# Four small reorderings in a fused attention and two-layer kernel: weight conversion at a step's end, softmax masks ahead of the divisions, some softmax copies on ScalarE

## The chip, the cores and the metric

The kernel runs on one core of a Trainium2 chip. The metric is device time in microseconds (us); lower is better. Times are given as the median of several executions, and one further execution was recorded by the hardware profiler. Engines are named as in the profile: PE is TensorE (matmuls), PEld its weight loads, DVE is VectorE, ACT is ScalarE, POOL is GpSimd, SP the engine that issues most DMAs.

## The reference

Causal attention with a running-sum bias, then two feed-forward layers. Shapes: 4 batches, 8 heads, 576 positions, 64 per head; 2304 tokens, model width 512, hidden width 2048.

```python
scores = scale * q @ k^T                       # per batch and head
bias = -(cum[:, :, :, None] - cum[:, :, None, :])   # cum: running sum of max(s, 0)
scores = where(causal, -1e9, scores + minimum(bias, 0))
attn = exp(scores - max); attn /= sum(attn) + 1e-9
x = attn @ v                                   # to 2304 x 512
h = maximum(x @ moe_w_in, 0);  x = h * h @ moe_w_out
h = x @ moe2_w_in;  out = (h * cos(h)) @ moe2_w_out
```

## The kernel before, in words

Tokens are cut into 9 blocks of 256. Attention of block k+1 runs beside the first feed-forward layer of block k. The layer of one block is 16 chunks; for each chunk `g1` multiplies the block by a slice of `w_in` (into the PSUM tile hps), `gact` makes relu and square on ACT, `grest` on DVE makes the low half gl, and `g2` multiplies by a slice of `w_out`. A call of `g1` or of `g2` is a slot, and slots alternate: g1 of chunk n, g2 of chunk n-2, g1 of chunk n+1. After the ninth block the second layer runs alone; the change does not touch it.

The order on every engine is the order in which `step` writes instructions down, and each engine works through its own in that order. One step handles one attention job i (one head, up to 128 query rows) at several stages of its life, and one to three slots. In order: ACT `x_high`; the first slot; ACT `prep_high` (the head two further on, raw to hi); DVE `evacuate` (three small operations a pair of heads: add, reciprocal, and the product that empties the PSUM tile pvs into xp); `softmax_tail`, which is `emit_mask(i - 1)` on DVE, then `emit_split(i - 2)` (a high copy p = sb * PSC, L650 on ACT or L652 on DVE, and a low part L656 on DVE); `x_low`, `grest`; `gact` of the first slot; `c_step`; DVE `prep_low`; PE `emit_qk(i)`; the further slots; ACT `emit_exp(i - 1)`; `turn` (PE transposes xp into the PSUM tile xps, and for a block's first pair DVE reduces a scale in `x_scale`, L769, that ACT's `x_high` of the next step reads); PE `emit_pv(i - 5)`; `c_total`; DMA transposes of p; loads.

`emit_qk` writes one of three PSUM buffers, and a job of 576 keys takes two, so that its second part needs the first mask of the job before it. The last block's attention (unit 8) is 16 such jobs, each a head of its own, in the steps that run beside the layer of blocks 6 and 7.

The layer's first three blocks use `w_in` as two fp32r halves; from the fourth (k = KC) on, as two fp16 halves. `c_step` converts it, chunk by chunk, during blocks 2 and 3: `c_add` (DVE, L872), then `c_high` (ACT, L878) at least two chunks of time later, then `c_low` (DVE, L883) in the next step. The times are chunk numbers t = `slots[0][1]`, the number of the next slot's chunk; `c_add(c)` is due at 33 + int(c * CONV_PACE). Before that, in blocks 1 and 2, `c_square` (ACT, L862) takes the power of each slice; after 12 and after 16 of them `c_total` has PE sum them over rows (L836, into a few columns of xps), and `c_scales` (DVE, L849 and three more) makes scales of the sum. The transposes, the value sums (`v_sum`, L453) and these sums all write the one tile xps, one PSUM bank.

`g1` of block 3 calls `c_step` itself where a slice is not converted yet.

Of the kernel before, what the change touches and what calls it, by code (L numbers as in the profile page):

```python
# [23 lines left out]
NF = DFF // 128  # L24
# [13 lines left out]
G2LAG = 2  # L38
PASSES = ((0, 0), (0, 1), (1, 0))
KC = 3  # L40
CONV_PACE = 1.7
SQ_A = 12


def _weave(*chains):

    chains = [iter(c) for c in chains if c is not None]
    while chains:
        for c in list(chains):
            if next(c, c) is c:  # L50
                chains.remove(c)
# [49 lines left out]
def _paired(head):  # L101

    return head[4] == [64]
# [29 lines left out]
def attention_moe_moe_kernel(  # L133
# [360 lines left out]
    def v_early():  # L494
        for f, g in vq[0] if vq else ():
            if f is v_scale:
                yield from f(g)
# [99 lines left out]
    def emit_exp(i):  # L597
        n, ti, q, r = jobs[i]
        h = heads[n][2]
        j = jd[i]  # L600
        x = h % 2
        if _paired(heads[n]):
            if x == 0:
                return
            r, x = 128, 0
        w, sb = j["w"], j["sb"]
        z = pd[n - h % 2]["z"]
        nc.scalar.activation(  # L608
            out=sb[0:r, 0:w], in_=sb[0:r, 0:w], func=ACTF.Exp, scale=-1.0, bias=j["nb"],
            accum_out=z[0:r, ti, x:x + 1],  # L610
        )
        if _paired(heads[n]):
            nc.scalar.copy(z[0:64, 0, 1:2], z[64:128, 0, 0:1])
# [16 lines left out]
    def emit_split(i):  # L630
        n, ti, q, r = jobs[i]
        j = jd[i]
        if _paired(heads[n]):
            if heads[n][2] % 2 == 0:
                return
            r = 128
        w, sb = j["w"], j["sb"]
        cw = 128 * ((w + 127) // 128)
        if n < EARLY:
            pp = j["ps"][0][0][:, BT:BT + cw]  # L640
            pt = at.tile([128, 640], F32, tag="pt", bufs=3, name="pt1")
            (nc.scalar.copy if ti else nc.vector.tensor_copy)(pt[:, 0:w], pp)
            j["pt"] = pt
            yield
            return
        p = p_tile(i)
        if cw > w:
            nc.gpsimd.memset(p[0:r, 0:2 * cw].rearrange("p (a c) -> p a c", a=2)[:, :, w:cw], 0.0)
        if 0 < cdone[1] and NF - 1 not in w16 and i % 2:
            nc.scalar.activation(out=p[0:r, 0:w], in_=sb[0:r, 0:w], func=ACTF.Copy, scale=PSC)  # L650
        else:
            nc.vector.tensor_scalar(  # L652
                out=p[0:r, 0:w], in0=sb[0:r, 0:w], scalar1=PSC, scalar2=None, op0=ALU.mult
            )
        yield
        nc.vector.scalar_tensor_tensor(  # L656
            out=p[0:r, cw:cw + w], in0=sb[0:r, 0:w], scalar=PSC, in1=p[0:r, 0:w],
            op0=ALU.mult, op1=ALU.subtract,
        )
        pt = at.tile([128, 1280], F16, tag="pt", bufs=3, name="pt")  # L660
        pt = pt[:, 0:2 * cw // 128 * r].rearrange("p (a r) -> p a r", r=r)
        turned.append((pt, p[0:r, 0:2 * cw]))
        if not last_block(i):
            p_turn()
        j["pt"] = pt
        if _paired(heads[n]):
            jd[i - 1]["pt"], j["pt"] = pt[:, :, 0:64], pt[:, :, 64:128]
        yield
# [221 lines left out]
    def c_step(t, last=None):  # L890


        for c in clow:
            c_low(c)
        clow.clear()
        while chigh and (chigh[0][1] + 2 <= t or last is not None and chigh[0][0] <= last):
            c, _ = chigh.pop(0)
            while clow:
                c_low(clow.pop(0))
            c_high(c)  # L900
            clow.append(c)
        if last is not None and last in clow:
            for c in clow:
                c_low(c)
            clow.clear()
        c_scales()
        n = 0
        while cdone[0] < NF and n < 1 and t >= (
            NF + 2 + cdone[0] if cdone[0] < SQ_A else 2 * NF + 2 + 2 * (cdone[0] - SQ_A)
        ):  # L910
            c_square(cdone[0])
            cdone[0] += 1
            n += 1
        while cdone[1] < cdone[2] and t >= (KC - 1) * NF + 1 + int(cdone[1] * CONV_PACE) and (
            cdone[1] not in (1, 2) or cdone[1] - 1 in w16 and cdone[1] - 1 not in w32
        ):
            c_add(cdone[1])
            chigh.append((cdone[1], t))
            cdone[1] += 1

    def c_total():
        if cdone[0] == SQ_A and SQ_A not in csent:
            csent.append(SQ_A)
            c_sums(0, SQ_A)
        elif cdone[0] == NF and NF not in csent:
            csent.append(NF)
            c_sums(SQ_A, NF)
# [12 lines left out]
    def job(i):  # L940
        return jobs[i] if 0 <= i < NJ else None
# [7 lines left out]
    def heads_ahead(i, *fs):  # L949
        if job(i) and jobs[i][1] == 0:  # L950
            for cnt, f, d in fs:
                upto(cnt, jobs[i][0] + d, f)
# [359 lines left out]
            stages[s] += 1  # L1312
            yield stages[s] - 1

    def softmax_tail(i):
        if job(i - 1):
            yield from emit_mask(i - 1)
        for j in stage(2, i - 2):
            yield from emit_split(j)
# [6 lines left out]
    def step(moe=0, bits=0, attn=True):  # L1326

        i = prog[0]
        held = len(xtq)
        prog[0] += attn  # L1330
        if attn:
            for j in stage(1, i - 2):
                emit_exp(j)
        x_high()
        if attn and job(i - 2):
            emit_turn(i - 2)
        if attn:
            heads_ahead(i, (next_, load_ext, 2))
        w_age()
        w_scales()  # L1340
        n = moe_slot() if moe else None
        slow = bool(vq) and any(f is v_wait for f, g in vq[0])
        if slow:
            v_sums()
        if attn:
            heads_ahead(i, (nhigh, prep_high, 2))
        _weave(evacuate())
        y_evict()
        if not attn or g2done[0] < 2:
            rests()  # L1350
        if xcq and xcq[-1][-1] and xcq[-1][0] == 1:
            x_low()
        _weave(softmax_tail(i) if attn else None, w_step(bits), None if slow else v_early())
        x_low()
        rests()
        w_lows()
        if attn and job(i - 1) and jobs[i - 1][0] < EARLY:
            for j in stage(1, i - 1):
                emit_exp(j)
        act(n)  # L1360
        if moe and slots and NF < slots[0][1] < (KC + 2) * NF:
            c_step(slots[0][1])
        if attn:
            heads_ahead(i, (nlow, prep_low, 2))
        if slow:
            _weave(v_early())
        if not (attn and last_block(i)):
            y_store()
        if attn and job(i):
            emit_qk(i)  # L1370
        if attn and last_block(i):
            heads_ahead(i, (nraw, load_raw, 4))
        for _ in range(moe - 1):
            act(moe_slot())
            y_evict()
        w_sums()
        if attn:
            for j in stage(1, i - 1):
                emit_exp(j)
        behind = any(job(j) and _paired(heads[jobs[j][0]]) for j in (i - 6, i - 5))  # L1380
        if attn and not behind:
            values(i)
        turn(held if moe and i > last_job[0] + TURN_FROM else len(xtq))
        if not slow:
            v_sums()
        if attn:
            for j in stage(3, i - LAG[0]):
                if j > i - lag(j):
                    stages[3] -= 1
                    break  # L1390
                emit_pv(j)
        if attn and behind:
            values(i)
        if moe:
            c_total()
        p_turn()
        w_ahead()
        if attn:
            heads_ahead(i, (nraw, load_raw, 4))
        v_late()  # L1400
        y_store()
        if later and prog[0] >= later[0][0]:
            later.pop(0)[1]()
# [45 lines left out]
    def w_step(n):  # L1449

        js = list(range(nw[2], min(nw[2] + n, wlim[0])))
        while wlow:
            w_lo(wlow.pop(0))
            yield
        w_squares()
        while wrest and not split(wrest[0]):
            w_rest(wrest.pop(0))
        if js:
            w_clip_to(js[-1])
            for _ in zip(*[w_bits(j) for j in js]):  # L1460
                yield
            for j in js:
                if wq[j][0] == 0:
                    wrest.append(j)
                else:
                    wbit.append(j)
            nw[2] += len(js)
# [495 lines left out]
```

## Time and profile before

| | us |
|---|---|
| median of 3 executions | 970.33 |
| lowest, highest | 970.06, 972.43 |
| the profiled execution | 972.91 |
| its span, first to last instruction | 970.8 |

The granted TensorE clock was 0.998 of full speed over the span. PE is busy for 97% of it. A busy matmul includes the time in which it flows through the array, so a PE that is always busy can still be late: matmuls are better read by the distance of their starts. Attention and the first layer take the span up to about 595 us, the second layer the rest. In the profile, waits and chains name the instruction that ended a wait.

### The profile page before, as it was taken

The page shows a single profiled execution, that of the slowest core. Times are in us where ns is not written, and L with a number is a line of the kernel's source. Part 1 is how long each engine was busy: PE and PEld are TensorE (multiplying, and loading weights), DVE is VectorE, ACT ScalarE, POOL GpSimd, SP SyncE. Part 2 cuts the span into 40 slices and gives each one's busy share as a digit, 9 for nine tenths or more (in the row PEclk, how much of TensorE's full clock was granted, in tenths as well). Part 3 has the DMA queues.
Part 4 walks back from the last instruction along what each step waited for, and adds up shares of the span by engine and source line. Part 5 has one row for each costly group of instructions (what it writes and reads, how often), then busy time and mean ns, then how long its engine had stood idle before and what let it go on. Part 6 is the DMA issues. An engine that isn't in the chain of part 4 may idle for free.

```text
span 970.8 us, 21039 instructions
## 1 busy us (share of the span) xinstructions
PE 937.3 (97%) x7474; PEld 726.9 (75%) x7474; DVE 769.7 (79%) x1944; ACT 709.7 (73%) x1625; POOL 159.9 (16%) x298
## 2 busy tenths in 40 slices
PE   6999999989999999999999999999999999999997
PEld 5899998988989988999989986445544456666664
DVE  6899986789798866787997375888788788798774
ACT  6799887878898767676776686677777666565553
POOL 2001123222211222222330022430000000001101
PEclk9999999999999999999999999999999999999999
DMA  8984799657998987589999679210000000112001
GB/s 246 312 271 149 168 213 227 168 145 151 200 183 191 204 195 170 134 177 174 211 215 158 217 267 362 66 44 23 1 1 1 22 1 22 49 60 67 23 22 66
DMA packets 158074, 135.38 MB, mean 139 GB/s; under 512 B 109272, under 2 KB 132128, under 8 KB 157968
## 3 DMA queue, kind: packets, MB, share of 16 engines
q1 hardware_dynamic: 147664, 123.78, 50.8%
q0 software_dynamic: 10304, 10.24, 5.2%
q8 instruction: 59, 0.97, 0.4%
q14 instruction: 47, 0.39, 0.1%
HBM read 93.91 MB, written 15.83 MB: 113 GB/s over the span
## 4 chain that ended last, share of the span: by engine, by line
PE 59%; DVE 6%; ACT 3%; issue 2%; DMA 2%; SPq 0%; DVEq 0%; ACTq 0%
PE o L1671 18%; PE hp L1610 12%; PE y L1197 11%; PE hps L1165 9%; PE bank L1762 5%; PE qkp L567 2%; PE pvs L697 2%; DVE k L415 1%; DVE sb L585 1%; DMA raw<-in_qk_dram 1%; DMA rw<-in_w_dram 1%; DMA vb<-v_d 1%; DVE wt L1678 1%; PE xps L752 0%; ACT sb L608 0%
## 5 line engine op out<-in xcount | busy, mean ns | idle before, releaser
L1197 PE MATMUL y<-gh,wt 128*128 128x256 f32 x1152 | 237.7, 289 | 0.0
L1197 PEld LDWEIGHTS y<-gh,wt 128*128 128x128 f32 x1152 | 188.6, 190 | 1.2
L1671 PE MATMUL o<-wt,gh 128*128 128x512 f16 x576 | 171.3, 379 | 1.5 <-ACT gh L1649 1.3
L1197 PE MATMUL y<-gl,wt 128*128 128x256 f32 x576 | 162.9, 283 | 0.5 <-DVE gl L1187 0.5
L1165 PE MATMUL hps<-xh,w 128*128 128x256 f16 x1152 | 142.0, 273 | 2.6 <-ACT g L1177 2.4
L1610 PE MATMUL hp<-yh,wt 128*128 128x512 f16 (+1 forms) x448 | 124.9, 348 | 0.0
L1165 PEld LDWEIGHTS <-w 128*128 128x128 f16 x1152 | 106.1, 98 | 17.8 <-issue 4.2
L1197 PEld LDWEIGHTS y<-gl,wt 128*128 128x128 f32 x576 | 109.9, 191 | 1.4 <-DVE gl L1187 0.9
L1671 PE MATMUL o<-wt,gl 128*128 128x512 f16 x288 | 109.2, 379 | 0.0
L1610 PEld LDWEIGHTS <-wt 128*128 128x128 f16 x672 | 63.9, 98 | 59.1
L1671 PEld LDWEIGHTS <-gh 128*128 128x128 f16 x576 | 56.3, 98 | 56.3 <-ACT gh L1649 1.6
L608 ACT ACTIVATE sb<-sb 128x128 f32<-128x128 f32 (+7 forms) x152 | 87.4, 575 | 4.9 <-DVE sb L585 4.3
L1177 ACT ACTIVATE g<-hps,sc 128x256 f32<-128x256 f32 x96 | 45.1, 470 | 61.3 <-PE hps L1165 59.8
L397 POOL DMA_DIRECT2D k<-ext_d x80 | 41.1, 514 | 260.2 <-PE qkp L567 159.3
L1165 PE MATMUL hps<-xh,wt 128*128 128x256 f32 x384 | 81.4, 294 | 0.3 <-ACT g L1179 0.2
L1187 DVE TENSOR_TENSOR gl<-g,gh 128x256 fp32r<-128x256 f32 x144 | 61.3, 426 | 22.8 <-ACT gh L1181 14.7
L1610 PE MATMUL hp<-yl,wt 128*128 128x512 f16 (+1 forms) x224 | 78.0, 348 | 0.0
L585 DVE CUSTOM_DVE_ANT_0 sb<-qkp,mask 128x128 f32<-128x128 f32 (+7 forms) x152 | 69.3, 456 | 5.3 <-PE qkp L552 4.3
L656 DVE SCALAR_TENSOR_TENSOR p<-sb,p 128x384 f16<-128x384 f32 (+3 forms) x120 | 66.3, 553 | 8.8 <-ACT p L650 5.6
L1635 ACT ACTIVATE a<-kf 128x512 f32<-128x512 f32 (+1 forms) x80 | 46.5, 583 | 31.4 <-DVE kf L1630 30.4
L405 ACT CAST hi<-raw 128x704 fp32r<-128x704 f32 (+2 forms) x80 | 58.8, 735 | 13.6 <-DMA raw<-in_qk_dram 7.2
L1165 PEld LDWEIGHTS hps<-xh,wt 128*128 128x128 f32 x384 | 64.5, 195 | 2.8 <-issue 1.2
(172 smaller groups left out, 2006.8 us busy)
## 6 DMA issues: line engine op xcount, KB each, us to landing
rw<-in_w_dram SPq DMA_DIRECT2D x64, 512.0 KB
raw<-in_qk_dram SPq DMA_DIRECT2D x48, 352.0 KB
yr<-y_d SPq DMA_DIRECT2D x17, 512.0 KB
raw<-in_qk_dram SPq DMA_DIRECT2D x16, 384.0 KB
v_d<-vt SPq DMA_DIRECT2D x16, 320.0 KB
vb<-v_d SPq DMA_DIRECT2D x32, 160.0 KB
vr<-in_v_dram POOLq DMA_DIRECT2D x15, 320.0 KB, 5.4
y_d<-yst SPq DMA_DIRECT2D x18, 256.0 KB
```

The source lines that it names most:

```text
L405: nc.scalar.copy(hi[:, BT - nq:BT + nk], raw[:, BT - nq:BT + nk])
L585: nc.vector.tensor_tensor_reduce(out=sb[0:r, c0:c0 + cn], in0=p[0:r, 0:cn], in1=mask[0:r, mo:mo + cn], scale=-0.125, scalar=(3.0e38 if k = ...
L608: nc.scalar.activation(out=sb[0:r, 0:w], in_=sb[0:r, 0:w], func=ACTF.Exp, scale=-1.0, bias=j["nb"], accum_out=z[0:r, ti, x:x + 1],)
L656: nc.vector.scalar_tensor_tensor(out=p[0:r, cw:cw + w], in0=sb[0:r, 0:w], scalar=PSC, in1=p[0:r, 0:w], op0=ALU.mult, op1=ALU.subtract,)
L1165: nc.tensor.matmul(hp, w[:, a, c * 128:(c + 1) * 128], (xh, xl)[e][:, c, :], start=(n == 0), stop=(n == 3 * KD - 1),)
L1177: nc.scalar.activation(out=g, in_=hp, func=ACTF.Relu, scale=hs1[:, f // 2:f // 2 + 1])
L1187: nc.vector.tensor_tensor(out=gl, in0=g, in1=gh, op=ALU.subtract)
L1197: nc.tensor.matmul(yps[k][d // 2][:, d % 2, :], w[:, a, d * 128:(d + 1) * 128], (gh, gl)[e], start=(f == 0 and n == 0 and d % 2 == 0), sto ...
L1610: nc.tensor.matmul(hp, chunk_of(w, a, c), (yh, yl)[e][:, c, :], start=(m == 0), stop=(m == 3 * KD - 1),)
L1635: nc.scalar.activation(out=a, in_=kf, func=ACTF.Sin, scale=-6.2831850)
L1671: nc.tensor.matmul(ops[j][a], (gh, gl)[e][:, a * 128:(a + 1) * 128], w[:, x, :], start=(first and m == 0), stop=(last and m == 2),)
L1762: nc.tensor.matmul(bank[b][:, 0:HB], w[:, a, wx, c * 128:(c + 1) * 128], y_side(j, yx, e, c), start=(start and n == 0), stop=(n == 5), ski ...
```

## The change

- `c_step` moves from behind the first slot's `gact` to behind the last slot and `emit_exp`, still ahead of `values`, `turn` and `emit_pv`; `c_total` moves from the end of a step to directly ahead of `c_step`, so the sum of the squares that a step's `c_step` completes is made one step later.
- `c_step` makes at most one `c_high` and one `c_add` a call (the wait of two chunks between them stays). `CONV_PACE` is 1.6 in place of 1.7. Since t is now read behind the last slot, the chunk numbers at which an operation falls due come one step earlier or later than before.
- In steps whose first slot is a g1 of block 1 or later, `emit_mask(i - 1)` stands ahead of `evacuate`.
- In the last block, the high copy of every odd job goes to ACT.

```diff
-CONV_PACE = 1.7
+CONV_PACE = 1.6
...
-        if 0 < cdone[1] and NF - 1 not in w16 and i % 2:
+        if i % 2 and (0 < cdone[1] and NF - 1 not in w16 or last_block(i)):
             nc.scalar.activation(out=p[0:r, 0:w], in_=sb[0:r, 0:w], func=ACTF.Copy, scale=PSC)
...
-        while chigh and (chigh[0][1] + 2 <= t or last is not None and chigh[0][0] <= last):
+        while chigh and (not clow and chigh[0][1] + 2 <= t or last is not None and chigh[0][0] <= last):
...
-        while cdone[1] < cdone[2] and t >= (KC - 1) * NF + 1 + int(cdone[1] * CONV_PACE) and (
+        if cdone[1] < cdone[2] and t >= (KC - 1) * NF + 1 + int(cdone[1] * CONV_PACE) and (
...
-    def softmax_tail(i):
-        if job(i - 1):
+    def softmax_tail(i, first):
+        if job(i - 1) and not first:
             yield from emit_mask(i - 1)
...
+        first = attn and job(i - 1) and n is not None and n >= NF
+        if first:
+            _weave(emit_mask(i - 1))
         _weave(evacuate())
...
-        _weave(softmax_tail(i) if attn else None, w_step(bits), None if slow else v_early())
+        _weave(softmax_tail(i, first) if attn else None, w_step(bits), None if slow else v_early())
...
         act(n)
-        if moe and slots and NF < slots[0][1] < (KC + 2) * NF:
-            c_step(slots[0][1])
...
         if attn:
             for j in stage(1, i - 1):
                 emit_exp(j)
+        if moe and slots and NF < slots[0][1] < (KC + 2) * NF:
+            c_total()
+            c_step(slots[0][1])
...
-        if moe:
-            c_total()
```

## Rows read from the trace of the kernel before

**Rows 1.** The page, busy time: share of the span, instructions.
```profile
PE 937.3 (97%) x7474; PEld 726.9 (75%) x7474; DVE 769.7 (79%) x1944; ACT 709.7 (73%) x1625; POOL 159.9 (16%) x298
```
**Rows 2.** Waits of PE, whole span: who released it, us, times, longest.
```profile
PE qkp L567 <- DVE sb L585: 3.0, 7, 0.7
...
PE pvs L697 <- DVE xp L737: 2.2, 3, 1.3
...
PE xps L836 <- ACT wj L862: 1.3, 1, 1.3
...
PE xps L752 <- DVE yss L849: 0.8, 1, 0.8
```
**Rows 3.** Timeline, 152 to 159 us: start, us, instruction, idle before and its releaser.
```profile
153.06 0.63 ACT L862 ACTIVATE wj<-wt 128x512 bf16<-128x512 f32 x1
...
155.74 0.46 DVE L652 TENSOR_SCALAR p<-sb 128x576 f16<-128x576 f32 x1 [0.69 <-ACT sb L608]
...
158.04 0.41 PE L567 MATMUL qkp<-hi 128*128 128x320 f32 x1 [0.92 <-DVE hi L412]
158.82 0.41 PE L567 MATMUL qkp<-k 68*128 68x320 f32 x1 [0.37 <-DVE k L415]
```
**Rows 4.** Timeline, 199 to 238 us, DVE and PE.
```profile
199.52 1.42 DVE L872 TENSOR_TENSOR w<-wt 128x512 f32<-128x512 f32 x2
...
201.59 0.23 DVE L652 TENSOR_SCALAR p<-sb 128x128 f16<-128x128 f32 x1 [0.38 <-DMA pt<-p]
...
207.76 0.16 PE L836 MATMUL xps<-yss,ones 128*128 128x4 bf16 x1 [1.26 <-ACT wj L862]
...
216.47 0.25 PE L697 MATMUL pvs<-vb,pt 128*128 128x64 f16 x3 [1.34 <-DVE xp L737]
...
237.74 0.54 PE L752 MATMUL xps<-ident,xp 128*128 128x128 f32 x2 [0.86 <-DVE vsc L462]
```
**Rows 5.** Groups by line, shapes apart: count, busy us, mean ns of one.
```profile
L652 DVE TENSOR_SCALAR p<-sb 128x576 f16<-128x576 f32 x24 | 11.0, 459 | 4.1 <-ACT sb L608 3.6 <-issue 0.3
...
L650 ACT ACTIVATE p<-sb 128x448 f16<-128x448 f32 x8 | 4.6, 570 | 0.3
...
L872 DVE TENSOR_TENSOR w<-wt 128x512 f32<-128x512 f32 x16 | 11.0, 686 | 0.1
...
L883 DVE SCALAR_TENSOR_TENSOR w<-w,sc,w 128x512 f16<-128x512 f32 x16 | 11.9, 743 | 0.1
...
L878 ACT ACTIVATE w<-w,sc 128x512 f16<-128x512 f32 x16 | 11.2, 714 | 0.0
...
L585 DVE CUSTOM_DVE_ANT_0 sb<-qkp,mask 128x128 f32<-128x128 f32 x32 | 8.9, 279 | 0.6 <-PE qkp L552 0.6
```
**Rows 6.** Timeline, 255 to 281 us, three engines.
```profile
258.05 0.15 DVE L769 TENSOR_REDUCE yss<-vsc 128x1 f32<-128x8 f32 x1
258.29 0.47 ACT L802 ACTIVATE xh<-xps,yss 128x256 f16<-128x256 f32 x1 [2.11 <-DVE yss L769]
...
263.46 1.47 PE L1165 MATMUL hps<-xh,w 128*128 128x256 f16 x12 [0.23 <-ACT g L1177]
...
280.20 0.42 PE L697 MATMUL pvs<-vb,pt 128*128 128x64 f16 x9 [0.70 <-DVE xp L737]
```
**Rows 7.** Waits of PE from 440 to 520 us.
```profile
PE qkp L567 <- DVE sb L585: 2.4, 6, 0.7
```
**Rows 8.** Stretches: length, busy us of PE, PEld, DVE, ACT, POOL; clock, DMA.
```profile
480.00:500.00 20.00, 19.11 (x204) 17.58 (x203) 18.30 (x56) 15.90 (x36) 6.16 (x15) 1.00 0.96 219
500.00:520.00 20.00, 18.92 (x225) 17.46 (x223) 18.60 (x56) 13.64 (x33) 4.25 (x12) 1.00 1.26 219
```
**Rows 9.** Timeline of the last unit's attention, ACT and DVE: three of six odd steps.
```profile
468.07 0.77 ACT L405 CAST hi<-raw 128x704 fp32r<-128x704 f32 x1
...
468.42 0.76 DVE L656 SCALAR_TENSOR_TENSOR p<-sb,p 128x576 f16<-128x576 f32 x1
...
494.67 0.76 ACT L405 CAST hi<-raw 128x704 fp32r<-128x704 f32 x1
...
495.35 0.76 DVE L656 SCALAR_TENSOR_TENSOR p<-sb,p 128x576 f16<-128x576 f32 x1
...
502.80 0.78 ACT L405 CAST hi<-raw 128x704 fp32r<-128x704 f32 x1 [2.29 <-DMA raw<-in_qk_dram]
...
503.20 0.76 DVE L656 SCALAR_TENSOR_TENSOR p<-sb,p 128x576 f16<-128x576 f32 x1
```

## The prediction

> **What bounds the kernel now.** I read the page's busy times first, then the waits of PE, then, stretch by stretch, the timeline at each wait, with the program's order beside it. PE is busy for 97% of the span [rows 1], so the change can only win what PE still loses to waits, and it can lose anything. The waits of PE that the four edits can reach are few: on masks, on the products that empty the value sums, and on the sums of squares [rows 2]. To these come waits on VectorE's low halves of the next head [rows 3], and one on the scales of the values [rows 4]. Together they are under 10 us, about 1%. Behind them DVE is nearly full: in 480 to 520 us it is busy for 18.3 and 18.6 of 20 us, ACT for 15.9 and 13.6, PE for 19.1 and 18.9, and the DMA share is about 1 [rows 8]. There DVE paces PE, so what counts is how long DVE works *and waits* per pair of steps; a mere order within a step doesn't change that.
>
> **Part 1, the squares behind the exponentials (block 1).** At 153.06 a square of 0.63 us stands on ACT ahead of a chunk's activation and of the exponential; DVE waits 0.69 for that exponential, then makes the low halves, and PE waits 0.92 and 0.37 for those [rows 3]. Behind the exponential, the square is off this chain: I take -0.6 (bounds 0 and -1.3). The first sum of squares now stands in the step after, behind the scale of the values, and the transposes behind it need DVE's reading of the sum in the same tile: that wait of 0.8 [rows 2] gets a round trip longer, +0.3 (bounds -0.8 to +0.4).
>
> What the rows show there: the transposes write other columns of xps than L849 reads, yet they wait for it [rows 2]. So the tile is guarded as a whole. The Trainium skill, PSUM — Partial Sum Buffer, section "PSUM bank collisions raise a hardware error", asks for the same: guard PSUM by bank, not by address. By that rule, which the trace agrees with, the second sum, moved behind the next step's `x_low`, must wait for `x_low` to read xps. The sum is as below with it; guarded by address the second sum would wait for nothing.
>
> **Part 2, conversion one at a time (blocks 2 and 3).** I counted from the code which operation falls into which step, before and after. By 237.74 both orders have made the same 9 additions (0.69 us) and 7 low halves (0.74) [rows 5], so DVE owes the same work; only its place changes. Before, a low half and two additions end at 200.94, ahead of a split that then waits for the transposes' DMA until 201.59 [rows 4]. After, the low half and one addition stand behind that split and the second addition a step later. So DVE enters the next steps late by about 1.4, plus a mask of 0.28 ahead of the division [rows 5], less the waits that it filled. The PE wait of 1.26 on the square [rows 4] goes, but PE then waits for `x_low`, and next for the division at 216.47, which DVE's work sets [rows 4]: I take +1.1 there. By 237.74, where PE now waits 0.86 for DVE [rows 4], most of it is back, since DVE's later waits are filled with work: +0.4 (bounds -2.6, both long waits gone, to +2.3).
>
> Block 3: at 258.05 DVE reduces the scale for which ACT has waited 2.11 [rows 6]. `c_step` comes before `turn`, and by my count this step now holds a low half and an addition where it held none: 1.43 us are put ahead of the reduction. ACT's chain from there on has no gap until PE's wait at 263.46 [rows 6]. One `c_high` of 0.71 [rows 5] is no longer in it, so PE is late by some 0.8. By 280.20 DVE has 1.4 less to convert, and PE's wait of 0.70 there [rows 6] goes: net +0.1 (bounds -0.9 to +1.5). Blocks 1 to 3 together: -0.6 + 0.3 + 0.4 + 0.1 = +0.2.
>
> **Part 3, masks ahead of the divisions.** A mask of 0.28 us [rows 5] or more now delays xp. PE waits on xp for its value sums in three places only [rows 2]; everywhere else that wait is absent and the first slot's matmuls hide the delay. Where they meet closely the mask adds to it: I count one place more than those of Part 2, in block 5, +0.3 (bounds 0 to +0.9). What it gives, an earlier mask for `emit_qk`, lies in the last unit and is counted there.
>
> **Part 4, the last unit's odd copies on ACT.** DVE loses eight copies of 0.46 [rows 5], 3.7 us; PE's six waits on masks there are 2.4 [rows 7]. This form isn't in the trace; ACT's copy of 448 takes 0.57, and the same per column would be 0.73 for 576; I take 0.66, nearer the row, since part of an instruction is fixed. (An estimate from the Trainium skill, ScalarE: Activation LUTs, section "What ACT_TABLE_LOAD costs", 186 ns and 0.833 a column, is 0.67, and 0.56 for the row's 448, which agrees.) But where does it stand? On ACT it follows `prep_high` (L405) of the same step, in these steps always one, since each job is a new head. The low part on DVE needs it. So per odd step I set "start of L405 + 0.77 + 0.66 - 0.08 of overlap" against the start of the low part now [rows 9]: 469.4 against 468.42, +1.0; 496.0 against 495.35, +0.7; 504.2 against 503.20, +1.0. The three pairs not shown give 0, +0.3, and once a saving of 0.5; the steps without `prep_high` save 0.5 once more. Sum +2.0. Further, the low halves that free a raw buffer come later, so the next raw load, for which ACT already waits 2.29 at 502.80 [rows 9], lands later too: +0.5. Since DVE paces PE here [rows 8], I count all: +2.5 (bounds -3.4, the copies all saved, to +3.6, no saving kept).
>
> **Sum.** +0.2 + 0.3 + 2.5 = +3.0. The profiled execution (972.91, its span 970.8) would take 975.9; it lies 2.6 above the median of the runs, and the same +3.0 on the median of 970.33 gives 973.3.
>
> **Rivals.** *Faster:* ACT's copy is ready when DVE has done mask and division, so DVE's 3.7 us are saved, the six waits of 2.4 [rows 7] go, and the masks ahead of the divisions do their part; with Part 1's -0.6 and about -0.9 in blocks 2 and 3, -3.9: 966.4. It decides at one point: whether L405 starts before DVE's second mask ends. For it speaks ACT's room (13.6 to 15.9 of 20 [rows 8]); against it that L405 is itself held by raw loads [rows 9] and that ACT works in order. *No change to be measured:* the copies save in some odd steps what they cost in others, Part 4 gives 0, the rest +0.5: 970.8. The sum's product then only trades its wait on the square for one on `x_low`, which is also the way in which the change would not do what it says. *Slower:* the forecast; it is a new wait, DVE on ACT's high copy, behind `prep_high`, in place of PE's waits on masks.
>
> **Chances.** A measurement of this kernel can tell about 0.3%, 2.9 us, from no change. The forecast, slower, 0.40; no change 0.36; faster 0.24. The unknown costs' bounds add up to far more than they would all reach together; the range takes the faster case down to its own time and the slower one to Part 4's upper end with about 2.5 of the other parts': 966.4 to 977.0. The slower case alone would be 971.5 to 977.0.
>
> **What would show it.** In the timeline after, between 465 and 520 us: L656 on DVE with an idle time ended by ACT p L650, in odd steps, of 0.5 to 1.2 us, and PE still waiting on masks in the even steps behind them. At about 258 us, L769 some 1.4 later behind L883 and L872. L836's second instance waiting for DVE's L825 and not for L862. At 158 us PE's wait shorter by 0.6. The prediction is wrong if L656 there waits for nothing (then the last unit gains 2 to 3 us), or if DVE has idle time in 199 to 240 us that my count does not see.

## The result, and the profile after

The changed kernel takes 976.5 us, median of 9 executions (973.9 to 979.6), beside 970.06 (969.5 to 972.6) of the kernel before on the same chip: a ratio of 1.0055, 95% interval 1.0042 to 1.0068, or +5.3 us. (The two medians lie 6.4 apart; this text goes by the ratio and its interval.) Forecast was "slower" with 973.3 in a range of 966.4 to 977.0. So the sign was right and the time lies in the range, close to its upper end. But the reason was not: the step that carried the forecast (the last unit, +2.5) cost nothing that can be measured, and the conversion in blocks 2 and 3, put at +0.5, makes nearly all of the loss. That the time falls into the range is luck.

Of the profiled execution (978.98, span 977.1) first the busy times, which answer to [rows 1], then the waits of PE over the whole span, which answer to [rows 2].

```profile
PE 938.8 (96%) x7474; PEld 727.7 (74%) x7474; DVE 765.8 (78%) x1935; ACT 714.0 (73%) x1634; POOL 159.7 (16%) x298
```
```profile
PE hps L1165 <- ACT g L1177: 4.0, 5, 1.3
PE pvs L697 <- DVE xp L737: 2.5, 3, 1.4
PE xps L836 <- ACT gh L1181: 2.3, 1, 2.3
...
PE qkp L567 <- DVE sb L585: 1.5, 3, 0.6
PE qkp L567 <- DMA k<-in_qk_dram: 1.4, 1, 1.4
...
PE xps L453 <- ACT x L808: 0.8, 1, 0.8
...
PE pvs L697 <- DMA pt<-p: 0.7, 1, 0.7
```

The work is the same and DVE has 4 us less of it, yet the span is longer. The masks' waits halve (3.0 to 1.5), which is what the edits aim at; the sum of the squares (L836) waits 2.3 in place of 1.3, the waits for g (L1177) grow from 2.4 in before to 4.0, and waits for x (L808) and for two DMAs appear. To see where, I took the start of the first g1 matmul of each block in both timelines; the differences are the lengths of the blocks:

```
                    first g1   block 1   block 2   block 3   blocks 4 to 7   rest
before              42.0       69.3      69.0      58.2      243.1           427.3
changed kernel      42.8       66.8      72.9      61.2      244.7           426.6
conversion's edits  42.0       68.8      71.9      60.0      244.5           426.1
```
(Block 0 takes 61.9, 62.0 and 61.2.) Blocks 2 and 3, in which the conversion runs, lose 4.0 and 2.9 us; block 1 gains 2.5; blocks 4 to 7, with the last unit, lose 1.6 in all. These are single profiles: blocks 4 to 7 take 242.3 to 246.0 over all fourteen, so 1.6 there says nothing.

Some of that is the clock of TensorE and must be set aside first. The time windows below (PE busy and its matmuls, granted clock, DMA share, GB/s) are of before around its waits at 158 us [rows 3], and of after around the second sum.

```profile
156.00:160.00 4.00, 2.71 (x18) 1.00 0.99 261
160.00:164.00 4.00, 4.00 (x31) 0.57 1.06 287
164.00:168.00 4.00, 3.79 (x29) 1.00 0.85 178
```
```profile
206.00:209.00 3.00, 3.00 (x31) 1.00 0.53 120
209.00:213.00 4.00, 1.81 (x14) 0.99 0.39 86
213.00:216.00 3.00, 2.87 (x16) 0.50 0.36 95
216.00:219.00 3.00, 3.00 (x28) 0.95 0.43 131
```

Behind PE's waits the clock falls from 2.4 to 1.2 GHz (granted 0.50) for about 3.4 us, in before in block 1, in after in block 2; 16 matmuls then start in 3 us where 31 did. At half speed 3.4 us lose about 1.7. Ahead of the last two us each of the two profiles holds one such stretch, so their difference of 6.3 us in the span is not the clock, but it moves 1.7 from block 1 to block 2. Without it block 1 gains 0.8, block 2 loses 2.3 and block 3 loses 2.9. The 0.8 is within chance: with the copies alone and with one each and the pace at the old place, whose block 1 is that of before, it takes 66.5 and 67.5, where before without its stretch takes 67.6.

What starts block 2's loss stands at its beginning. DVE of after, then the first three PE waits of the block that are not in before, from the timeline:

```profile
177.73 0.69 DVE L872 TENSOR_TENSOR w<-wt 128x512 f32<-128x512 f32 x1 [3.71 <-DMA pt<-p]
178.34 0.88 DVE L482 SCALAR_TENSOR_TENSOR vt<-vr,vsc,vt 128x640 f16<-128x640 f32 x1
179.14 0.48 DVE L585 CUSTOM_DVE_ANT_0 sb<-qkp,mask 128x320 f32<-128x320 f32 x1
```
```profile
185.87 0.38 PE L1165 MATMUL hps<-xh,wt 128*128 128x256 f32 x1 [0.87 <-ACT g L1179]
188.63 0.16 PE L453 MATMUL xps<-ss,ones 128*128 128x1 bf16 x1 [0.84 <-ACT x L808]
195.23 0.25 PE L697 MATMUL pvs<-vb,pt 128*128 128x64 f16 x3 [1.39 <-DVE xp L737]
```

The first addition, `c_add(0)`, waits 3.71 us for a DMA, and everything of DVE stands behind it: the low half of v, then the mask. The exponential on ACT waits for that mask, and from there ACT has hardly a gap up to the chunk's g (L1179, 185.44 us) for which PE waits 0.87:

```profile
180.31 0.78 ACT L608 ACTIVATE sb<-sb 128x576 f32<-128x576 f32 x1 [2.21 <-DVE sb L585]
...
183.42 0.67 ACT L650 ACTIVATE p<-sb 128x576 f16<-128x576 f32 x1
```

The second of these lines is another effect of the early addition. By its test on `cdone[1]`, `emit_split` gives the high copy of an odd job to ACT as soon as one addition has been made. So job 55's copy, which DVE makes in before (182.08, 0.46 us), went to ACT here, ahead of that g, and DVE waits 1.22 for it. In the profiles this copy is on ACT in just the kernels whose first addition is early. Counted from the start of block 2, that g comes 2.8 us later than with the first addition later (an experiment below); some 0.6 of this is the copy, the rest the late mask.

In before the low half of v and the mask are

```profile
175.49 0.87 DVE L482 SCALAR_TENSOR_TENSOR vt<-vr,vsc,vt 128x640 f16<-128x640 f32 x1
176.29 0.47 DVE L585 CUSTOM_DVE_ANT_0 sb<-qkp,mask 128x320 f32<-128x320 f32 x1
...
183.58 0.69 DVE L872 TENSOR_TENSOR w<-wt 128x512 f32<-128x512 f32 x1
```

and the addition comes two steps later and waits for nothing. The reason is in the code. `c_add` of the first slices puts its sum into the tile p3, which `p_tile` lends to every third job's p as long as no addition has been made. In step 55 job 53 writes that tile (L652, L656), and its transposes' DMA reads it until 177.7. `c_add(0)` is due at chunk 33; read behind the first slot, that is first true in step 57; read behind the last one, in step 55. So a due time that nobody changed came two steps earlier (the description of the change speaks of one), into a step in which the tile is still in use.

The second loss is the sum that the diff moves on purpose. PE's weight load and matmul of it:

```profile
213.13 0.11 PEld L836 LDWEIGHTS <-ones 128*128 128x128 bf16 x1 [2.58 <-DVE xh L825]
213.13 0.19 PE L836 MATMUL xps<-yss,ones 128*128 128x4 bf16 x1 [2.33 <-ACT gh L1181]
```

The list of waits names ACT's gh for it, which ended just then by chance; the load ahead of it shows the true one, DVE's reading of xps in `x_low`. The third is in block 3, DVE, ACT and PE:

```profile
259.77 0.39 DVE L652 TENSOR_SCALAR p<-sb 128x320 f16<-128x320 f32 x1 [2.84 <-DMA pt<-p]
...
262.05 0.74 DVE L883 SCALAR_TENSOR_TENSOR w<-w,sc,w 128x512 f16<-128x512 f32 x1
...
262.71 0.68 DVE L872 TENSOR_TENSOR w<-wt 128x512 f32<-128x512 f32 x1
263.31 0.15 DVE L769 TENSOR_REDUCE yss<-vsc 128x1 f32<-128x8 f32 x1
...
263.56 0.47 ACT L802 ACTIVATE xh<-xps,yss 128x256 f16<-128x256 f32 x1 [2.85 <-DVE yss L769]
...
264.91 0.81 PE L1165 MATMUL hps<-xh,w 128*128 128x256 f16 x6 [1.27 <-ACT g L1177]
```

Beside [rows 6] it is plain: a low half and an addition stand ahead of the reduction, and g1 waits 1.27 where it waited 0.23. That is 1.0 of block 3's 2.9. PE's other waits in this block are 1.36 for the load of a later head's k, 0.68 for a transposed p and 0.5 for xp, 3.8 us with g1's, where before has 0.9 in all (0.70 for xp and 0.23 for g). So the two DMAs that came late make 2.0. The wait for a load of k is in most of the profiles (0.3 with one each and the pace at the old place, 0.8 with the masks alone, in this block), so its size in a single profile is no measure of the edit.

### The profile page after: what moved, and what is told of

Same layout as the page of the kernel before. It is cut to its first block, busy times and chain, and to the rows that moved or that the text cites. A ratio compares the mean times of both kernels' runs of the same rounds, so it can differ in the third digit from the quotient of the medians.

```text
span 977.1 us, 21071 instructions
## 1 busy us (share of the span) xinstructions
PE 938.8 (96%) x7474; PEld 727.7 (74%) x7474; DVE 765.8 (78%) x1935; ACT 714.0 (73%) x1634; POOL 159.7 (16%) x298
## 5 line engine op out<-in xcount | busy, mean ns | idle before, releaser
L1177 ACT ACTIVATE g<-hps,sc 128x256 f32<-128x256 f32 x96 | 45.1, 470 | 60.1 <-PE hps L1165 59.2
L656 DVE SCALAR_TENSOR_TENSOR p<-sb,p 128x384 f16<-128x384 f32 (+3 forms) x120 | 66.2, 552 | 16.0 <-ACT p L650 13.1
```

The costliest lines, as they stand in the source:

```text
L656: nc.vector.scalar_tensor_tensor(out=p[0:r, cw:cw + w], in0=sb[0:r, 0:w], scalar=PSC, in1=p[0:r, 0:w], op0=ALU.mult, op1=ALU.subtract,)
L1177: nc.scalar.activation(out=g, in_=hp, func=ACTF.Relu, scale=hs1[:, f // 2:f // 2 + 1])
```

## The experiments

All were timed in five rounds beside the kernel before. First the change was taken apart, each part by itself in the kernel before.

**The copies alone.**
```diff
-        if 0 < cdone[1] and NF - 1 not in w16 and i % 2:
+        if i % 2 and (0 < cdone[1] and NF - 1 not in w16 or last_block(i)):
```


> The kernel before with one edit alone: the odd high copies of the last block on ScalarE. The prediction's Part 4 gives +2.5 us (0.26%). The rival from the trace of after: the starts of the layer's chunks lose only about 0.5 to 1 us between 480 and 560 us, so +0.0 to +1.0. If it is faster by 2 us or more, the copies are a gain that the rest of the change hides.

Measured: 0.9992 (0.9979 to 1.0005), -0.8 us. Groups of instructions between 440 and 525 us (count, busy, mean ns, idle ahead of it), the windows that answer to [rows 8] (PE, PEld, DVE, ACT, POOL, clock, DMA), and PE's waits that answer to [rows 7]:

```profile
L656 DVE SCALAR_TENSOR_TENSOR p<-sb,p 128x576 f16<-128x576 f32 x16 | 12.1, 758 | 5.6 <-ACT p L650 5.3
L650 ACT ACTIVATE p<-sb 128x576 f16<-128x576 f32 x8 | 5.4, 680 | 0.4 <-DMA pt<-p 0.4
```
```profile
480.00:500.00 20.00, 19.32 (x213) 17.60 (x212) 17.15 (x53) 16.51 (x38) 5.99 (x15) 1.00 1.04 235
500.00:520.00 20.00, 19.31 (x217) 18.00 (x216) 18.21 (x56) 15.37 (x34) 4.26 (x12) 1.00 1.11 213
```
```profile
PE qkp L567 <- DVE sb L585: 1.6, 4, 0.5
PE qkp L567 <- DVE k L415: 0.5, 2, 0.3
```

The wait that was forecast is there, five times, 1.1 us on the mean (0.35 to 1.87), and costs nothing that can be measured: DVE is busy 1.5 us less in the forty and PE's waits go from 2.4 to 2.1. In the profiles a small cost may be seen: blocks 6 and 7, which run beside the last unit, take 118.9 to 119.2 us in the three kernels with the copies and 118.2 to 119.0 in the eleven without.

**The masks alone.**
```diff
-        if job(i - 1):
+        if job(i - 1) and not first:
             yield from emit_mask(i - 1)
...
+        first = attn and job(i - 1) and n is not None and n >= NF
+        if first:
+            _weave(emit_mask(i - 1))
         _weave(evacuate())
```


> The kernel before with one edit alone: the masks ahead of the divisions. The prediction's Part 3 gives +0.3 us. Rival: the trace of after has two waits of PE on xp in blocks 2 and 3 (1.39 and 0.55 us) that before has at other places; if the masks make them, this kernel loses 1.5 to 2.5 us.

Measured: 0.9999 (0.9986 to 1.0013), -0.1 us: no effect that can be measured. PE waits 0.31 us for xp at the place where after waits 1.39, and 0.32 with the conversion's edits alone; in these profiles it is 1.39 only with both.

**The conversion's edits alone**: place, one each, and pace, that is the diffs of the two kernels that follow, together.

> The kernel before with the conversion's edits alone: c_step and c_total at the new place, one of each a call, pace 1.6. My theory after reading both traces: the loss of 5.3 us is here, +4 to +6 us (blocks 2 and 3 lose about 7, block 1 gains 2). The prediction's Parts 1 and 2 give -0.1 to +0.2.

Measured: 1.0051 (1.0035 to 1.0068), +5.0 us: within the noise the whole loss of the change.

**The place alone.**
```diff
-        if moe and slots and NF < slots[0][1] < (KC + 2) * NF:
-            c_step(slots[0][1])
...
+        if moe and slots and NF < slots[0][1] < (KC + 2) * NF:
+            c_total()
+            c_step(slots[0][1])
...
-        if moe:
-            c_total()
```


> The kernel before with the new place of c_step and c_total alone, pace 1.7 and as many operations a call as are due. If the place makes the loss (VectorE's low halves and additions ahead of the products and the scales that PE waits for), +4 to +6 us, as the conversion's edits together. If one operation each and the pace make it, 0 to +1 us here, or even a gain of 1 to 2 from block 1.

Measured: 1.0121 (1.0102 to 1.0141), +11.8 us, over twice the loss of the three together, and the addition waits 3.65 for the transposes here too. Here block 3 takes 64.5 us; PE waits there, 240 to 312 us:

```profile
PE hps L1165 <- DVE w L883: 2.6, 1, 2.6
PE hps L1165 <- ACT g L1177: 1.3, 2, 1.1
```

The last low halves come too late for the chunks that need them; behind this wait, and behind one of 3.02 for the second sum, the clock is at half for 3.4 and 6.8 us.

**One each and the pace, at the old place.**
```diff
-CONV_PACE = 1.7
+CONV_PACE = 1.6
...
-        while chigh and (chigh[0][1] + 2 <= t or last is not None and chigh[0][0] <= last):
+        while chigh and (not clow and chigh[0][1] + 2 <= t or last is not None and chigh[0][0] <= last):
...
-        while cdone[1] < cdone[2] and t >= (KC - 1) * NF + 1 + int(cdone[1] * CONV_PACE) and (
+        if cdone[1] < cdone[2] and t >= (KC - 1) * NF + 1 + int(cdone[1] * CONV_PACE) and (
```


> The kernel before with one operation of each kind a call and pace 1.6, c_step and c_total at their old places. The place alone lost 1.21%, place, one each and pace together 0.51%, so these two win 0.7% behind the new place. If they are good by themselves, -1 to -3 us here; if they only mend what the place breaks (the late low halves for which block 3's last chunks waited 2.64 us), -0.5 to +1.0.

Measured: 1.0002 (0.9988 to 1.0016). They gain nothing by themselves; they mend what the place breaks at block 3's end. The place is the cause: without it there is no loss.

Then three ways to move less.

**The sum at its old place**, in the conversion's edits.
```diff
         if moe and slots and NF < slots[0][1] < (KC + 2) * NF:
-            c_total()
             c_step(slots[0][1])
...
+        if moe:
+            c_total()
         p_turn()
```


> The conversion's edits with c_total left at the end of its step. My theory: the second sum's wait of 2.32 us for x_low falls to the 1.2 to 1.5 us for the square, and with it the stretch at half clock behind it (212.9 to 216.2 us in after) goes: 2 to 3 us less than the conversion's edits together, that is +2 to +3 us against before. Rival: VectorE's order sets the time there, the wait only moves to the value sums: +4.5 to +5.5 us, no gain.

Measured: 1.0040 (1.0028 to 1.0053), 1.1 us less than with it, where 2 to 3 were expected. (Each of these differences between two kernels is uncertain by about 2 us, so this one isn't clear of noise.) The second sum's wait falls to 1.38, but the first sum now waits for its square, which the new place puts late in the step; PE's waits from 160 to 215 us and the windows:

```profile
PE xps L836 <- ACT wj L862: 3.4, 2, 2.0
```
```profile
170.00:174.00 4.00, 2.99 (x14) 0.57 0.09 31
174.00:178.00 4.00, 4.00 (x21) 0.58 0.34 64
208.00:211.00 3.00, 1.62 (x18) 1.00 0.32 58
211.00:215.00 4.00, 4.00 (x24) 0.57 0.40 111
```

So for the first sum the later step is right (0.54 in after), and the test is spoilt for the second one.

**The conversion behind `turn`**, in the conversion's edits; `c_total` stays ahead of `turn`.
```diff
-            c_step(slots[0][1])
...
         if not slow:
             v_sums()
+        if moe and slots and NF < slots[0][1] < (KC + 2) * NF:
+            c_step(slots[0][1])
```


> The conversion's edits with c_step behind turn and the value sums in place of ahead of them, c_total left ahead of turn. If the reduction of the scale behind a low half and an addition makes block 3's loss (g1's wait of 1.27 us at 262 us), this wait goes back to some 0.2 us and the kernel is at +3.5 to +4.2 us. If the loss of block 3 has another cause (the transposes' DMA and the loads that come later), +4.8 to +5.5 us.

Measured: 1.0027 (1.0010 to 1.0045), 2.4 us less than ahead of it, where the theory for block 3 gave 0.8 to 1.5. In the profile block 3's wait is gone. But the profile doesn't prove the theory: here the transposes' DMA, for which L652 waits 2.84 us in after, came in time. Issues of the transposes by SP's queue, from before, after and this kernel:

```profile
252.83 6.18 SPq L628 DMA_TRANSPOSE pt<-p  x2
```
```profile
255.96 7.42 SPq L628 DMA_TRANSPOSE pt<-p  x2
```
```profile
253.38 4.93 SPq L628 DMA_TRANSPOSE pt<-p  x2
```

With c_step ahead of turn and the DMA in time (the sum at its old place, 4.95), block 3 took 58.2 us, no more than before; with the DMA late and nothing ahead of the reduction (before) it took 58.2 too. Apart from the place alone, the loss of about 2 us or more in block 3 is there in these profiles only where both come together.

**Only the squares of block 1 moved**, with their sum; the rest as in before.
```diff
-        if moe and slots and NF < slots[0][1] < (KC + 2) * NF:
+        if moe and slots and 2 * NF <= slots[0][1] < (KC + 2) * NF:
             c_step(slots[0][1])
...
+        if moe and slots and NF < slots[0][1] < 2 * NF:
+            c_total()
+            c_step(slots[0][1])
...
-        if moe:
+        if moe and slots and slots[0][1] >= 2 * NF:
             c_total()
```


> The kernel before with c_step and c_total at the new place in block 1 alone (the first twelve squares and their sum), everything from block 2 on at the old place and pace. By the prediction's Part 1, -0.3 us (-0.6 and +0.3). By the trace of before, in which the clock is at half from 160.7 to 164.0 us behind the waits of 0.92 and 0.37 us that the square makes, -1.5 to -2.5 us where that happens: it would then beat both kernels.

Measured: 0.9999 (0.9984 to 1.0015). Part 1 by itself is worth nothing that can be measured, and the gain hoped for from the clock didn't come.

Last, the two waits that the trace of after shows were taken away one at a time, then both together with the place behind `turn`, and the first was put into the kernel before.

**The first addition later**, in the conversion's edits.
```diff
-        if cdone[1] < cdone[2] and t >= (KC - 1) * NF + 1 + int(cdone[1] * CONV_PACE) and (
+        if cdone[1] < cdone[2] and t >= (KC - 1) * NF + (1 + int(cdone[1] * CONV_PACE) if cdone[1] else 2) and (
```


> The conversion's edits with the first addition alone due a chunk later (step 57 in place of 55, as in before). Theory: in the trace of after VectorE waits 3.71 us in that addition, for the transposes' DMA that still reads its tile, and masks, exponentials, copies and the layer's first chunks of block 2 are late behind it (PE waits of 0.87, 0.84 and 0.32 us between 184 and 194 us). Without it these waits go: 2 to 3 us less than the conversion's edits together, +2 to +3 us against before. Rival: those waits come from the squares and high copies that now follow the exponentials on ScalarE; then no gain, +4.5 to +5.5 us.

Measured: 1.0009 (0.9992 to 1.0027), +0.9 us: one addition, two steps later (its halves follow it), takes back 4.1 of the 5.0. It waits for nothing now, job 55's copy is back on DVE, the waits at the head of block 2 are gone, block 2 takes 68.3 us and block 3 58.0. The 4.1 isn't the price of the wait alone: of the 5.1 between the two profiles' spans, block 2 has 3.7, of which 1.7 is the half-clock stretch behind the second sum that is absent here, and block 3 has 2.1, with its transposes in time (5.03). The longest of PE's waits that are left from 171 to 241 us:

```profile
PE xps L836 <- ACT gh L1181: 2.1, 1, 2.1
PE pvs L697 <- DVE xp L737: 1.0, 1, 1.0
```

**The second sum another step later**, in the conversion's edits; `pend` is whether a reading of xps was still due at the step's start.
```diff
+        pend = bool(xcq)
...
-            c_total()
+            if cdone[0] < NF or not pend:
+                c_total()
```


> The conversion's edits with the second sum of the squares held back by one more step (68 in place of 67), since in 67 it stands behind x_low's reading of the same tile. Theory: PE's wait of 2.32 us goes and with it the stretch at half clock behind it (3.3 us, 1.65 us lost): 2 to 4 us less than the conversion's edits together, +1 to +3 us against before. Rival: PE waits as long for the value sums behind it; +4.5 to +5.5 us.

Measured: 1.0019 (1.0000 to 1.0038), +1.8 us. Both held in part: the sum waits 0.47, and the value sums behind it wait 1.73, where before has 1.34 [rows 4]. The first addition is still early here and waits 3.76, but there is no half-clock stretch, and block 3 takes 58.5:

```profile
212.86 0.18 PE L836 MATMUL xps<-yss,ones 128*128 128x4 bf16 x1 [0.47 <-ACT gh L1181]
218.35 0.25 PE L697 MATMUL pvs<-vb,pt 128*128 128x64 f16 x3 [1.73 <-DVE xp L737]
```

**The changed kernel with three mends.**
```diff
-        if cdone[1] < cdone[2] and t >= (KC - 1) * NF + 1 + int(cdone[1] * CONV_PACE) and (
+        if cdone[1] < cdone[2] and t >= (KC - 1) * NF + (1 + int(cdone[1] * CONV_PACE) if cdone[1] else 2) and (
...
+        pend = bool(xcq)
...
-            c_total()
-            c_step(slots[0][1])
+            if cdone[0] < NF or not pend:
+                c_total()
...
             v_sums()
+        if moe and slots and NF < slots[0][1] < (KC + 2) * NF:
+            c_step(slots[0][1])
```


> The changed kernel with three mends: the first addition a chunk later, the second sum a step later, c_step behind turn and the value sums. If the three waits are the whole loss, it stands at the kernel before, -1.5 to +0.7 us; if the new place costs by itself, +2 us or more.

Measured: 1.0017 (0.9999 to 1.0034), +1.7 us. Two thirds of the loss are gone and no gain comes out; none of these kernels is measurably faster than the one before. The gains don't add up: one at a time, in the conversion's edits, the three mends give 4.1, 3.2 and 2.4, nearly twice the loss of 5.0. Each of them also rids the profile of the half-clock stretch and of block 3's loss, so these two hang on when things happen, and not on one of the moves alone.

**The first addition early, in the kernel before.**
```diff
-        while cdone[1] < cdone[2] and t >= (KC - 1) * NF + 1 + int(cdone[1] * CONV_PACE) and (
+        while cdone[1] < cdone[2] and t >= (KC - 1) * NF + (1 + int(cdone[1] * CONV_PACE) if cdone[1] else -2) and (
```


> The kernel before with the first addition alone made early (step 55 in place of 57; its high and low halves follow at 57 and 58 in place of 60 and 61), all else at the old places. If VectorE's wait for the transposes' DMA is what block 2 loses, it shows here by itself: a wait of some 3 us in that addition, and +2 to +3 us. Rival: the wait is absorbed, within 0.5 us of before.

Measured: 1.0059 (1.0037 to 1.0082), +5.7 us, as much as the whole change. DVE, PE, and the windows:

```profile
179.31 0.69 DVE L872 TENSOR_TENSOR w<-wt 128x512 f32<-128x512 f32 x1 [4.55 <-DMA pt<-p]
180.03 0.36 DVE L412 TENSOR_TENSOR hi<-raw,hi 64x192 fp32r<-64x192 f32 x1
```
```profile
180.44 0.45 PE L567 MATMUL qkp<-hi 128*128 128x256 f32 x1 [2.11 <-DVE hi L412]
```
```profile
176.00:180.00 4.00, 2.33 (x20) 1.00 0.64 137
180.00:184.00 4.00, 3.56 (x36) 0.58 0.47 141
184.00:188.00 4.00, 4.00 (x23) 0.57 0.58 181
```

At the old place the low half that `emit_qk` needs stands right behind the addition, so PE waits 2.11, and the clock stays at half for about 7 us, some 3.5 lost. Removed, the early addition gives back 4.1; put in alone, it costs 5.7, twice what was expected. So taken out, it takes most of the loss with it, and put in alone it is enough for one of this size. That its wait for the DMA does all this isn't shown: job 55's copy goes to ACT and back with it, and 3.5 of the 5.7 here, like 1.7 of the 4.1 there, is the clock. Nor is the loss always this large where it is early: with the second sum later it was 1.8, with the conversion behind `turn` 2.6.

## Why the prediction was right in sign and wrong in its reasons

**Part 4 (+2.5) is the step that came out too high.** The new wait of DVE on ACT's copy came as described: 5.3 us in all, less the 3.7 of the copies that DVE no longer makes, is 1.6 net where +2.0 were counted. Single waits went from 0.35 to 1.87 where 0.5 to 1.2 were named. The copy took 0.68, by [rows 5] put at 0.66. The Trainium skill, ScalarE: Activation LUTs, section "What ACT_TABLE_LOAD costs", gives an estimate of 0.67, which the trace agrees with. What failed is "Since DVE paces PE here [rows 8], I count all". DVE waits 5.3 us for copies and PE waits no longer for masks and low halves than before, so most of it was slack: busy for 18.5 of 20 us was taken for a pace. The result was that of the rival "no change", in which the copies save in some steps what they cost in others.

**Part 2 (+0.4 and +0.1) is the step that came out too low.** "DVE owes the same work; only its place changes" is true of the durations and false of the waits. I listed in which step each operation falls, but not what each waits for at its new step, nor what else in the code reads the count of additions. The count also began at 199 us, at the first waits of PE; the first moved addition starts some 22 us earlier. Within the counted stretch the sign named at the end came true: from 201 to 242 us DVE waits 4.5 us for ACT's high copies, where before waits 1.9 from 199 to 240. The bound of +2.3 for block 2 holds only with the half clock taken out (4.0 with it); block 3's 2.9 lies outside its +1.5. There the step that was priced, the reduction behind a low half and an addition, came near its price: g1's wait grew by 1.0 where 0.8 were taken. What was put at nothing is that two DMAs would land later; they make the other 2.0 in that profile.

**What was right in Part 2.** The second sum waits for `x_low`, and longer than it waited for the square: 2.33 against 1.26. That this is +1.07 and +1.1 was taken is luck: the +1.1 was to hold for this wait and the division behind it, and that division's wait (1.34 at 216.47 [rows 4]) isn't in after, while one of 1.39 at 195 us is new. The sum writes other columns of xps than L825 reads, and its weight load waited 2.58 for it, so the program guards the tile as a whole, as the prediction said. The Trainium skill, PSUM — Partial Sum Buffer, section "PSUM bank collisions raise a hardware error", asks for such a guard; the trace agrees. L769 is later as announced, but by more: counted from the start of block 3 it comes 2.8 us later than in before (18.7 against 15.9), 1.4 of it for L883 and L872.

**Part 1 (-0.3).** PE's wait at 158 us goes from 0.92 and 0.37 to 0.37, as taken. But the edit isn't shown to do it: with the copies alone, whose block 1 is that of before, it is 0.37 too, and with the first addition early, where block 1 is also that of before, 1.28 and 0.37. So the -0.6 was read from a wait that comes and goes between executions. Not seen: at 116 us a square now stands ahead of a chunk's activation and PE waits 0.65. The squares alone measured nothing. The profile of before also had the clock at half behind 158 us, so beside it block 1 of after looks 1.7 us better than the edit made it.

**Part 3 (+0.3).** Measured alone it is -0.1 (-1.4 to +1.3), which doesn't speak against its bounds of 0 to 0.9; the masks' waits do get fewer, and nothing that can be measured follows from it.

**The range.** Its upper end isn't the sum that its sentence names: 970.33 + 3.6 + about 2.5 is 976.4 and not 977.0, and with 976.4 the measured 976.5 would lie at the very edge.

**What stays open.** Why the transposes in block 3 took 5.9 and 7.4 us with the conversion's edits and in after, and 4.9 to 5.1 in the others with the new place, while before had 6.2 and no loss; how the early addition's wait and job 55's copy share what they cost; whether the place behind `turn` gains by the reduction or by the sum behind it; and why the three mends leave 1.7 us (-0.1 to +3.3) in the median, while their profile's span, 968.3, is shorter than that of before; the profiled execution was the fastest of the twelve, and the interval holds zero.

## What to carry to other kernels

When an instruction moves in an in-order queue, look up for each moved one which tile it writes and who still reads it at the new step, before adding up durations; a borrowed buffer is the first to check. A due time that is read at another point of the step is an edit of the schedule even where its number stays. That an engine is busy for over 90% doesn't make it the pace: ask what PE waits for, and how long the engine's own waits could grow first. And a wait that one profile shows isn't yet a price: look whether a kernel with the same code there has it too.

## What the runs showed of the hardware

The clock of TensorE fell to 1.2 GHz behind single waits of PE: of 2.33 us in after and 2.3 with the conversion's edits, of 3.02 and 2.64 with the place alone, of 2.01 and 1.38 with the sum at its old place, of 1.55 with the squares alone, of 2.11 with the early addition, and of 0.92 and 0.37 close together in before (1.28 and 0.37 at the same place with the early addition). It didn't fall behind 2.32 us with the place behind `turn`, nor behind 2.08 with the first addition later, nor behind 1.26 in before. So the length of the wait alone doesn't decide, and what does isn't settled here. These stretches lasted from 3.4 us to about 7, and cost about half their length on top of the wait (an estimate from the granted 0.50). In two profiles, of the masks alone and of the squares alone, the clock was at half from 24 to 45 us, a stage that no edit touches. Over all executions the granted clock of after (0.996 to 0.998) and of before beside the first four experiments (0.988 to 1.000, median 0.998) is alike, so in the medians it explains no difference between the two.
